# Scatters into the first layer's table without an order among themselves, each behind the next chunk's products on GpSimd

## The chip, the cores and the metric

The kernel runs on one core of a Trainium2 chip. The metric is the device time of one execution in microseconds (us). A profile of one execution stands beside the timed runs; its times count from the start of its span. TensorE is called PE here, VectorE DVE, ScalarE ACT, GpSimd POOL and SyncE SP, as in the profile.

## What is computed

A decayed linear attention over 2 x 768 tokens feeds two mixture-of-experts layers, each with eight experts and one expert per token. The reference, cut to what matters:

```python
attn_out = _attn_ref(q, k, v, lam)                 # blocks of tokens, a running state per head
x = attn_out.transpose(0, 2, 1, 3).reshape(B * S, H * D)      # 1536 x 512
# first layer
xn = x / (norm(x) + 1e-6); en = expert_emb / (norm(expert_emb) + 1e-6)
logits = xn @ en.T / tau
expert_idx = argmax(logits, axis=1)
gate_w = softmax(logits)[arange(N), expert_idx]
for e in range(8):
    mask = expert_idx == e
    h = maximum(x[mask] @ w1[e], 0)                # 512 -> 1024
    out[mask] = gate_w[mask, None] * (h @ w2[e])   # 1024 -> 512
# second layer: the same with its own weights and logits = x @ w_gate
```

## The kernel before

**Attention, in steps.** A loop over `s` from 0 to 11 takes the tokens in chunks of 128 (two batches in turn). The code is written out as a hand-made software pipeline, and every engine runs its instructions in the order in which the code emits them. In step `s`, `st_A(s)` puts the products of keys and queries on PE (line 420), `st_pool(s)` puts three products on POOL (`qd` L433, the decayed queries; `kd` L437, the decayed keys; `ds` L444, the decayed state), `st_mask(s)` applies the decay mask on DVE, `st_B(s - 1)` multiplies on PE with `qd` of the chunk before (L456) and with the masked products (L461), and `st_S(s - 1)` updates the state (L475, L481). So POOL's `qd` of chunk 6 is wanted by PE in step 7. The chunk's finished rows go to a table `xd` in device memory (`st_rows`, L501, an SP transfer).

**Routing, inside the steps.** `st_lT`, `st_pick` and `st_rank` compute for each token of an earlier chunk its expert and its place in that expert's list (`posk`). Every third step from 5 on (steps 5, 8, 11) `Gates` makes the gate values of three chunks on ACT and DVE, and then `scat(it)` (L550) writes for each of the three chunks 128 records of two words, token number and gate, to rows `posk[:, it]` of the table `tab1` in device memory. It is an indirect transfer that POOL issues. The framework sees three writes into one tensor and makes each wait for the one before; the wait stands on POOL. The scatters of chunks 9 to 11 (`LATE`) come after the loop.

**Who reads the table.** `tb0` (L615, SP) loads the first 216 rows of the first expert at the end of step 11. The tokens of chunks 9 to 11 reach the first expert by matrix products (`late_in`, L584), the others by gathers of `xd` with `tb0` (L636, POOL), which PE transposes (L655). The other experts' rows come by `load_x` (L747, SP) and `gather` (L768, POOL), transposed by `x_in` (L788).

**Weights.** SP loads the experts' weights in pieces of 512 KB (`raw`, L354) into five buffers. ACT makes the upper part `whi` (L361), and DVE or POOL the rest (`wlo` L379, `wlr` L373). In the attention steps a piece is loaded at the end of a step and converted by ACT at the end of the next.

**A helper of the second layer.** `put` declares that a scatter has no dependence on the scatters before it, keeps it in a list, and puts a one-element `memset` of `gap` behind it on POOL. `after_puts` makes a reader of the table wait for all of that list. Before the change only scatters into the second layer's table (L960) use them.

Of the kernel before, what the change touches and what calls it, by code (L numbers as in the profile page):

```python
# [75 lines left out]
def body(ctx, tc, nc, A, O):  # L76
# [5 lines left out]
    tab1 = dram.tile([E * TS, 2], I32, name="tab1")  # L82
    tab2 = dram.tile([E * TS, 3], I32, name="tab2")
    F_d = dram.tile([8, 256], F32, name="F_d")
    tab1_e = tab1.rearrange("(e n) r -> e n r", e=E)
# [6 lines left out]
    rec1 = const.tile([128, 12, 2], I32, name="rec1")  # L92
# [9 lines left out]
    posk = const.tile([128, 12], I32, name="posk")  # L102
# [97 lines left out]
    for g in range(2):  # L200
        nc.sync.dma_start(
            out=Dm[:, 4 * g:4 * g + 4, :],
            in_=bass.AP(tensor=f0.tensor, offset=f0.offset + 256 * g, ap=[[1, 128], [512, 4], [1, 128]]))
    load_X(1, 1)
    qtab = ac.tile([128, 4, 128], F32, name="qtab")
    for hh in range(2):
        nc.sync.dma_start(out=qtab[64 * hh:64 * hh + 64],
                          in_=bass.AP(tensor=f0.tensor, offset=f0.offset + 256 * hh + 128,
                                      ap=[[0, 64], [512, 4], [1, 128]]))
# [60 lines left out]
        nc.vector.tensor_copy(out=enT[:, :, 0:8], in_=pe)  # L270


    puts = []
    gap = const.tile([1, 1], F32, name="gap")

    def put(inst):

        for p in puts:
            tc.declare_no_dep(inst.ins, p.ins, reason="distinct rows")
        puts.append(inst)  # L280
        nc.gpsimd.memset(gap, 0.0)

    def after_puts(inst):
        for p in puts:
            tc.add_manual_dep(inst.ins, p.ins.name, mybir.DependencyInfo(mybir.DependencyClass.Sync, mybir.DependencyReason.DATA), reason="rows of the table")

    def route_pick(lg, n, nb, inv=None):
# [140 lines left out]
    def st_pool(it):  # L428
        b, c = it % 2, it // 2
        X = Xs[it]  # L430
        if c > 0:
            qd = wk.tile([128, 4, 128], F32, tag="qd", name="qd")
            nc.gpsimd.tensor_tensor(out=qd, in0=X[:, 0, :].rearrange("p (a i) -> p a i", a=4), in1=qtab, op=ALU.mult)  # L433
            qds[it] = qd
        if c < 5:
            kd = wk.tile([128, 512], F32, tag="kd", name="kd")
            nc.gpsimd.tensor_tensor(  # L437
                out=kd.rearrange("p (a g d) -> p g a d", g=2, d=64),
                in0=X[:, 2, :].rearrange("p (a g d) -> p g a d", g=2, d=64),
                in1=Dm[:, :, 127:128].rearrange("p (g a) o -> p g a o", g=2).to_broadcast([128, 2, 4, 64]), op=ALU.mult)  # L440
            kds[it] = kd
        if 0 < c < 5:
            ds = wk.tile([128, 4, 64], F32, tag="ds", name="ds")
            nc.gpsimd.tensor_tensor(out=ds, in0=state[b][c % 2], in1=qtab[:, :, 127:128].to_broadcast([128, 4, 64]),  # L444
                                    op=ALU.mult)
            dss[it] = ds
# [100 lines left out]
            route_gate(self.sh, 128, self.n, rec1[:, self.s, 1:2].bitcast(F32))  # L547

    def scat(it):
        nc.gpsimd.indirect_dma_start(out=tab1[:, :], out_offset=bass.IndirectOffsetOnAxis(ap=posk[:, it:it + 1], axis=0),  # L550
                                     in_=rec1[:, it, :], in_offset=None)

    lTs = {}
    Ps = {}
# [10 lines left out]
    W0, nb0 = W1S[0], nblk(W1S[0])  # L565
    n0 = W0 // nb0
# [17 lines left out]
            nc.tensor.matmul(pt0[k // 2][:, k % 2, :], xrs[it][:, 128 * k:128 * k + 128], Ps[it],  # L584
                             start=(it == LATE[0] and k % 2 == 0), stop=False)

    gates = None
    for s in range(12):
        ps = psf[s] if s < 2 else st_A(s)
        st_pool(s)  # L590
        if s >= 3:
            st_rank(s - 3)
        if s >= 5 and s % 3 == 2:
            gates = Gates(s - 5, s - 2)
        st_mask(s, ps, 0)
        st_mask(s, ps, 1)
        if s >= 2:
            st_lT(s - 2)
            st_rows(s - 2)
        if gates:  # L600
            gates.shift()
            gates.exp()
        if s >= 1:
            st_B(s - 1)
            st_S(s - 1)
        if gates:
            gates.gate()
            for it in range(s - 5, s - 2):
                scat(it)
            gates = None  # L610
        if s >= 2:
            st_pick(s - 2)
        if s == 11:
            tb0 = sm.tile([n0, nb0, 2], I32, tag="tb0", name="tb0", bufs=1)
            nc.sync.dma_start(out=tb0, in_=tab1_e[0, 0:W0, :].rearrange("(j p) c -> p j c", p=n0))  # L615
        if 1 <= s and s + 3 < 12:
            load_X(s + 3)
        if s == 1:
            init_dram()
        if s >= 5:  # L620
            wcur.load(s - 5)
        for g in LO_AT.get(s, ()):
            wcur.split_lo(g)
        if 6 <= s < 11:
            wcur.split_hi(wcur.todo.pop(0))
# [22 lines left out]
    gates = Gates(9, 12)  # L648
# [78 lines left out]
    class Expert:  # L727
# [12 lines left out]
        def load_x(self):  # L740
            n, nb, W = self.n, self.nb, self.W
            self.tb = sm.tile([n, nb, self.nc_], I32, tag="tb", name="tb", bufs=4)
            if isinstance(self.e, int):
                src = self.tab[self.e, 0:W, :].rearrange("(j p) c -> p j c", p=n)
            else:
                src = self.tab[bass.ds(self.e, 1), 0:W, :].rearrange("a (j p) c -> p (a j) c", p=n)
            i = nc.sync.dma_start(out=self.tb, in_=src)  # L747
            if self.second:
                after_puts(i)
            self.gate = self.tb[:, :, self.nc_ - 1:self.nc_].bitcast(F32)  # L750

        def begin(self):
# [576 lines left out]
```

## Time and profile before

| | us |
|---|---|
| median of 3 runs | 499.51 (494.91 to 502.37) |
| the profiled execution, its own time | 493.88 |
| its span, first to last instruction | 492.1 |
| PE busy | 433.0 (88% of the span) |
| DVE busy | 336.9 (68%) |
| ACT busy | 269.7 (55%) |
| POOL busy | 226.1 (46%) |

The time of the profiled execution is its span and 1.8 us around it. Busy time is that of compute instructions alone; an engine that waits in its queue counts as idle. The steps of the attention take about the first 92 us, the experts the rest.

### The profile page before, as it was taken

To read this page: it belongs to the slowest core of one execution; us is meant where nothing else is said; L and a number is where in the kernel's file an instruction comes from. 1 tells how busy PE (TensorE), PEld (TensorE's weight loads), DVE (VectorE), ACT (ScalarE), POOL (GpSimd) and SP (SyncE) were. 2 spreads that over 40 slices of the span, in tenths; PEclk is the share of its full clock that TensorE was granted. 3 is DMA by queue.
4 is the path that set the end of the run, shared out by engine and by line. 5 is a ranking of instruction groups with operands and counts; after the bars stand their busy time and mean duration, and the time that the engine had idled before them with its cause. 6 is when DMAs were issued, how large, how long until landed. Compare 5 with 4: busy or idle time off the path is not lost. (4 is left out here: it accounts for less than half of the span.)

```text
span 492.1 us, 9560 instructions
## 1 busy us (share of the span) xinstructions
PE 433.0 (88%) x3482; PEld 375.2 (76%) x3484; DVE 336.9 (68%) x714; ACT 269.7 (55%) x443; POOL 226.1 (46%) x224
## 2 busy tenths in 40 slices
PE   7696577759699999999999898999999999999980
PEld 3585566549578898988888797878987788988970
DVE  5454282525569888989888966853858588989950
ACT  2244253404467575665767445645768585776830
POOL 4641725415262738375574634403435725545520
PEclk9999697978899999999999999999999999999996
DMA  6998283231958485867658246483767767786400
GB/s 199 338 345 291 96 291 75 52 125 10 356 173 281 159 283 168 286 188 264 221 190 277 85 170 206 139 259 129 260 213 247 268 206 250 245 265 244 152 25 15
DMA packets 36693, 99.00 MB, mean 201 GB/s; under 512 B 10524, under 2 KB 12068, under 8 KB 35617
## 3 DMA queue, kind: packets, MB, share of 16 engines
q1 hardware_dynamic: 31569, 88.02, 53.7%
q0 software_dynamic: 4768, 10.28, 6.7%
q8 instruction: 29, 0.48, 0.4%
q14 instruction: 23, 0.19, 0.1%
q10 hardware_dynamic: 304, 0.03, 0.0%
HBM read 87.65 MB, written 11.21 MB: 201 GB/s over the span
## 5 line engine op out<-in xcount | busy, mean ns | idle before, releaser
L379 DVE SCALAR_TENSOR_TENSOR wlo<-raw,whi 128x1024 f16<-128x1024 f32 x98 | 128.8, 1316 | 33.0 <-ACT whi L361 32.1
L361 ACT ACTIVATE whi<-raw 128x1024 fp32r<-128x1024 f32 x128 | 131.3, 1050 | 5.2 <-DMA raw<-in_wa_dram 5.2
L373 POOL TENSOR_TENSOR wlr<-raw,whi 128x1024 fp32r<-128x1024 f32 x30 | 73.7, 2457 | 112.3 <-ACT whi L361 90.1
L795 PE MATMUL pm<-xT,whi 128*128 128x416 f32 (+8 forms) x416 | 99.2, 364 | 6.7 <-DVE xT L577 3.2
L795 PE MATMUL pm<-ht,whi 128*128 128x416 f32 (+7 forms) x384 | 86.7, 362 | 0.0
L795 PEld LDWEIGHTS pm<-xT,whi 128*128 128x128 f32 x416 | 68.8, 189 | 12.4 <-DVE xT L577 5.1
L795 PEld LDWEIGHTS pm<-ht,whi 128*128 128x128 f32 x384 | 66.8, 191 | 2.0
L801 PEld LDWEIGHTS <-wlo 128*128 128x128 f16 x720 | 57.2, 98 | 14.0 <-issue 8.6
L801 PE MATMUL pm<-xH,wlo 128*128 128x208 f16 (+11 forms) x512 | 59.4, 259 | 0.6 <-DVE xH L580 0.6
L845 ACT ACTIVATE ht<-t 128x416 fp32r<-128x416 f32 (+11 forms) x64 | 35.9, 561 | 27.4 <-DVE t L839 27.1
L851 DVE SCALAR_TENSOR_TENSOR ht<-t,ht 128x416 fp32r<-128x416 f32 (+11 forms) x64 | 42.6, 666 | 7.9 <-ACT ht L845 7.9
L838 ACT ACTIVATE t<-pm 128x416 f32<-128x416 f32 (+8 forms) x52 | 26.3, 506 | 33.9 <-PE pm L795 33.7
L839 DVE SCALAR_TENSOR_TENSOR t<-pm,t 128x416 f32<-128x416 f32 (+8 forms) x52 | 29.7, 571 | 14.8 <-ACT t L838 14.1
L960 POOL DMA_INDIRECT tab<-rec,pi x16 | 27.8, 1739 | 21.1 <-issue 7.3
L550 POOL DMA_INDIRECT tab<-rec,posk x12 | 11.9, 995 | 46.9 <-DMA tab<-rec,posk 25.4
L801 PE MATMUL pm<-ht,wlr 128*128 128x208 f32 (+8 forms) x208 | 33.4, 282 | 0.0
L967 POOL DMA_INDIRECT out_y_dram<-yr,tb x17 | 19.3, 1137 | 30.0 <-ACT yr L928 21.5
L574 ACT ACTIVATE xT<-pt 128x384 fp32r<-128x384 f32 (+9 forms) x33 | 16.8, 513 | 23.8 <-PE pt L788 11.9
L801 PEld LDWEIGHTS pm<-ht,wlr 128*128 128x128 f32 x208 | 29.1, 190 | 0.4
L768 POOL DMA_INDIRECT xr<-y2d,tb x17 | 24.1, 1416 | 9.3 <-issue 7.5
L801 PE MATMUL pm<-hh,wlo 128*128 128x208 f16 (+8 forms) x208 | 26.2, 256 | 0.0
L768 POOL DMA_INDIRECT xr<-xd,tb x14 | 23.4, 1670 | 4.4 <-issue 3.1
(197 smaller groups left out, 715.5 us busy)
## 6 DMA issues: line engine op xcount, KB each, us to landing
raw<-in_wa_dram SPq DMA_DIRECT2D x64, 512.0 KB, 5.5
raw<-in_wb_dram SPq DMA_DIRECT2D x64, 512.0 KB, 4.1
X<-in_att_dram SPq DMA_DIRECT2D x8, 1024.0 KB, 7.7
X<-in_att_dram SPq DMA_DIRECT2D x8, 512.0 KB, 6.1
xd<-xr SPq DMA_DIRECT2D x12, 256.0 KB, 4.6
y2d<-yr SPq DMA_DIRECT2D x2, 416.0 KB
y2d<-yr SPq DMA_DIRECT2D x2, 384.0 KB, 3.3
Dm<-F_d SPq DMA_DIRECT2D x2, 256.0 KB
```

Source lines behind the costliest of these rows:

```text
L361: nc.scalar.activation(out=f, in_=self.raw[g], func=AF.Copy, scale=self.scale(g))
L373: (nc.gpsimd if self.pat[g] == "p" else nc.vector).tensor_tensor(out=t.rearrange("p a b -> p (a b)"), in0=self.raw[g], in1=self.hi[g].rear ...
L379: nc.vector.scalar_tensor_tensor(out=t.rearrange("p a b -> p (a b)"), in0=self.raw[g], scalar=SW, in1=self.hi[g].rearrange("p a b -> p (a ...
L768: nc.gpsimd.indirect_dma_start(out=xr[0:n], out_offset=None, in_=self.rows, in_offset=bass.IndirectOffsetOnAxis(ap=idx[:, j, 0:1], axis=0))
L795: nc.tensor.matmul(pm[:, j, 0:2 * W].rearrange("p (a w) -> p a w", a=2), wh, s2, start=first, stop=last)
L801: nc.tensor.matmul(pm[:, j, 0:self.W], wl, sh, start=False, stop=False)
L838: nc.scalar.activation(out=t1, in_=pm[:, :, W:2 * W], func=AF.Copy, scale=sc)
L839: nc.vector.scalar_tensor_tensor(out=t2, in0=pm[:, :, 0:W], scalar=sc, in1=t1, op0=ALU.mult, op1=ALU.add)
L845: nc.scalar.activation(out=ht[:, :, 0, :], in_=t2, func=AF.Relu)
L851: nc.vector.scalar_tensor_tensor(out=ht[:, :, 1, :], in0=t2, scalar=0.0, in1=ht[:, :, 0, :].bitcast(F32), op0=ALU.max, op1=ALU.subtract)
L960: i = nc.gpsimd.indirect_dma_start(out=tab2[:, :], out_offset=bass.IndirectOffsetOnAxis(ap=self.pi[:, j:j + 1], axis=0), in_=rec2[0:n, rb[ ...
L967: i = nc.gpsimd.indirect_dma_start(out=O["y"], out_offset=bass.IndirectOffsetOnAxis(ap=self.tb[:, j, 1:2], axis=0), in_=self.yr[0:n, j, :] ...
```

## The change

The scatters into `tab1` go through `put` with a list of their own (`puts1`), so they don't wait for one another, and a `gap` memset stands behind each. The three scatters of a group are no longer issued together in the step in which their gates are made: they are put in a list `ready`, and each of the next three steps issues one, behind that step's `st_pool`. In step 11 those that are left are issued on the spot. `tb0` and every later load of rows of `tab1` wait for all scatters issued by then.

```diff
-    puts = []
+    puts, puts1 = [], []
     gap = const.tile([1, 1], F32, name="gap")
-    def put(inst):
-        for p in puts:
+    def put(inst, to=puts):
+        for p in to:
             tc.declare_no_dep(inst.ins, p.ins, reason="distinct rows")
-        puts.append(inst)
+        to.append(inst)
         nc.gpsimd.memset(gap, 0.0)
...
     def scat(it):
-        nc.gpsimd.indirect_dma_start(out=tab1[:, :], out_offset=bass.IndirectOffsetOnAxis(ap=posk[:, it:it + 1], axis=0),
-                                     in_=rec1[:, it, :], in_offset=None)
+        put(nc.gpsimd.indirect_dma_start(
+            out=tab1[:, :], out_offset=bass.IndirectOffsetOnAxis(ap=posk[:, it:it + 1], axis=0),
+            in_=rec1[:, it, :], in_offset=None), puts1)
...
-    gates = None
+    gates, ready = None, []
     for s in range(12):
         ps = psf[s] if s < 2 else st_A(s)
         st_pool(s)
+        if ready:
+            scat(ready.pop(0))
...
             gates.gate()
-            for it in range(s - 5, s - 2):
-                scat(it)
+            ready += range(s - 5, s - 2)
             gates = None
+            while s == 11 and ready:
+                scat(ready.pop(0))
...
-            nc.sync.dma_start(out=tb0, in_=tab1_e[0, 0:W0, :].rearrange("(j p) c -> p j c", p=n0))
+            after_puts(nc.sync.dma_start(out=tb0, in_=tab1_e[0, 0:W0, :].rearrange("(j p) c -> p j c", p=n0)), puts1)
...
             i = nc.sync.dma_start(out=self.tb, in_=src)
-            if self.second:
-                after_puts(i)
+            after_puts(i, puts if self.second else puts1)
```

The instructions of PE, DVE and ACT and their order stay as they were. Three places show what moves. The first is POOL's queue from the end of step 5 to step 8 before the change; `tab` is the table, `rec` the records, `DMASW` the semaphores of POOL's own transfers.

```order
L444 TENSOR_TENSOR ds<-st_183,qtab 128x256 [waits DVE_49]
L550 DMA tab_62<-rec_69,posk 13312x2 [waits DVE_49]
L550 DMA tab_62<-rec_69,posk 13312x2 [waits DMASW0_49]
L550 DMA tab_62<-rec_69,posk 13312x2 [waits DMASW1_49]
L433 TENSOR_TENSOR qd<-X,qtab 128x512 [waits DMAHW4_49,PE_49,Pool_49]
L437 TENSOR_TENSOR kd<-X,Dm 128x2x4x64 [waits PE_49,Pool_49]
L444 TENSOR_TENSOR ds<-st_182,qtab 128x256 [waits Pool_49]
```

The same engine and the same place after the change:

```order
L444 TENSOR_TENSOR ds<-st_183,qtab 128x256 [waits DVE_49]
L433 TENSOR_TENSOR qd<-X,qtab 128x512 [waits DMAHW4_49,PE_49,Pool_49]
L437 TENSOR_TENSOR kd<-X,Dm 128x2x4x64 [waits PE_49,Pool_49]
L444 TENSOR_TENSOR ds<-st_182,qtab 128x256 [waits DVE_49]
L550 DMA tab_62<-rec_69,posk 13312x2 [waits DVE_49]
L281 MEMSET gap 1x1
L433 TENSOR_TENSOR qd<-X,qtab 128x512 [waits DMAHW6_49,PE_49,Pool_49]
L437 TENSOR_TENSOR kd<-X,Dm 128x2x4x64 [waits PE_49,Pool_49]
L444 TENSOR_TENSOR ds<-st_184,qtab 128x256 [waits DVE_49]
L550 DMA tab_62<-rec_69,posk 13312x2
L281 MEMSET gap 1x1 [waits Pool_49]
```

The products of chunk 6 stood behind three scatters, of which two waited for a transfer; now they stand ahead of the first, and one scatter follows each chunk's products.

The second place is POOL's queue around the end of step 11, before the change; L636 is the first gather for the first expert, L373 a product of weights.

```order
L433 TENSOR_TENSOR qd<-X,qtab 128x512 [waits DMAHW1_49,PE_49,Pool_49]
L550 DMA tab_62<-rec_69,posk 13312x2 [waits DMASW5_49,DVE_49]
L550 DMA tab_62<-rec_69,posk 13312x2 [waits DMASW6_49]
L550 DMA tab_62<-rec_69,posk 13312x2 [waits DMASW7_49]
L373 TENSOR_TENSOR wlr<-raw,whi 128x1024 [waits DMAHW4_49,Activation_49]
L636 DMA xr<-xd,tb_1179 108x512 [waits DMAHW5_49,DMAHW3_49,DMAHW7_49,DMAHW2_49,DMAHW0_49]
```

After the change:

```order
L433 TENSOR_TENSOR qd<-X,qtab 128x512 [waits DMAHW1_49,PE_49]
L550 DMA tab_62<-rec_69,posk 13312x2
L281 MEMSET gap 1x1 [waits Pool_49]
L550 DMA tab_62<-rec_69,posk 13312x2 [waits DVE_49]
...
L550 DMA tab_62<-rec_69,posk 13312x2 [waits DMASW0_49]
...
L373 TENSOR_TENSOR wlr<-raw,whi 128x1024 [waits DMAHW4_49,Activation_49]
L640 DMA xr<-xd,tb_1188 108x512 [waits DMAHW3_49,DMAHW5_49,DMAHW2_49,DMAHW7_49,DMAHW0_49,DMASW1_49]
```

(Left out are the third group's second scatter, like the first row of its kind, and the `gap` rows.) The last scatter of the second group has come here, ahead of the third group, whose scatters now wait only for DVE and for transfers of much earlier scatters. The `LATE` scatters change in the same way, without moving.

The third place is SP's queue at the load of `tb0`, as a piece of the difference:

```order
 L354 DMA raw<-in_wa_dram 128x1024 [waits DMAHW6_49,DVE_49]
 L501 DMA xd<-xr 128x512 [waits DMAHW7_49,Activation_49]
-L615 DMA tb_1179<-tab_62 108x2x2 [waits DMAHW0_49,DMASW0_49]
+L619 DMA tb_1188<-tab_62 108x2x2 [waits DMASW5_49,DMASW4_49,DMASW6_49,DMASW3_49,DMASW7_49,DMASW2_49,DMAHW0_49,DMASW1_49,DMASW0_49]
 L354 DMA raw<-in_wa_dram 128x1024 [waits DMAHW1_49,DVE_49]
 L501 DMA xd<-xr 128x512 [waits DMAHW2_49,Activation_49]
```

It keeps its place, ahead of a load of weights and of the store of a chunk's rows, and waits for nine scatters in place of the last.

## Rows read from the trace of the kernel before

**Rows 1.** The page, part 2: TensorE's granted clock, 40 slices of 12.3 us.
```profile
PEclk9999697978899999999999999999999999999996
```

**Rows 2.** Waits from 20 to 125 us: who waited for whom, total, times, longest (us).
```profile
POOL tab L550 <- DMA tab<-rec,posk: 25.4, 8, 6.8
PE px L456 <- POOL qd L433: 14.3, 2, 9.5
```

**Rows 3.** Timeline of PE, 36 to 83 us: start, duration, instruction, idle ahead.
```profile
37.40 1.16 PE L420 MATMUL ps<-X 64*128 64x128 f32 x16
...
42.73 1.16 PE L420 MATMUL ps<-X 64*128 64x128 f32 x16
54.43 1.97 PE L456 MATMUL px<-qd,st 64*64 64x128 f32 x16 [9.46 <-POOL qd L433]
58.62 1.16 PE L420 MATMUL ps<-X 64*128 64x128 f32 x16
...
70.41 1.16 PE L420 MATMUL ps<-X 64*128 64x128 f32 x16
77.47 1.97 PE L456 MATMUL px<-qd,st 64*64 64x128 f32 x16 [4.83 <-POOL qd L433]
82.08 1.16 PE L420 MATMUL ps<-X 64*128 64x128 f32 x16
```

**Rows 4.** Timeline of POOL, 46 to 118 us.
```profile
46.45 0.96 POOL L550 DMA_INDIRECT tab<-rec,posk  x1 [6.79 <-DMA tab<-rec,posk]
52.12 0.97 POOL L550 DMA_INDIRECT tab<-rec,posk  x1 [4.70 <-DMA tab<-rec,posk]
53.10 1.27 POOL L433 TENSOR_TENSOR qd<-X,qtab 128x512 f32<-128x512 f32 x1
...
55.34 0.62 POOL L444 TENSOR_TENSOR ds<-st,qtab 128x256 f32<-128x256 f32 x1
...
87.38 1.01 POOL L550 DMA_INDIRECT tab<-rec,posk  x1 [5.93 <-DVE m L508]
...
92.21 0.97 POOL L550 DMA_INDIRECT tab<-rec,posk  x1 [1.44 <-DMA tab<-rec,posk]
...
100.77 1.05 POOL L636 DMA_INDIRECT xr<-xd,tb  x1 [5.20 <-issue]
...
111.82 1.00 POOL L550 DMA_INDIRECT tab<-rec,posk  x1 [8.70 <-DVE cm L694]
...
117.87 0.97 POOL L550 DMA_INDIRECT tab<-rec,posk  x1 [2.32 <-DMA tab<-rec,posk]
```

**Rows 5.** Timeline of SP's queue: the loads of table rows.
```profile
94.34 0.34 SPq L615 DMA_DIRECT2D tb<-tab  x1
...
120.03 0.41 SPq L747 DMA_DIRECT2D tb<-tab  x1
```

**Rows 6.** Timeline of PE: the first transposes of gathered rows.
```profile
104.37 0.69 PE L655 MATMUL pt<-ident,xr 108*128 108x108 f32 x4 [4.16 <-DMA xr<-xd,tb]
...
132.20 0.84 PE L788 MATMUL pt<-ident,xr 117*128 117x117 f32 x4 [4.63 <-DMA xr<-xd,tb]
```

**Rows 7.** Stretches: busy us (instructions) of each engine, clock, DMA share, GB/s.
```profile
40.00:50.00 10.00, 4.97 (x80) 4.13 (x80) 3.26 (x13) 4.34 (x9) 0.96 (x1) 0.86 0.91 297
50.00:60.00 10.00, 5.57 (x74) 5.01 (x76) 1.43 (x6) 1.93 (x4) 7.86 (x9) 0.63 0.10 33
132.00:136.00 4.00, 3.80 (x15) 3.51 (x16) 1.47 (x3) 0.98 (x2) 0.00 (x0) 0.57 0.95 354
```

**Rows 8.** Timeline of POOL, 158 to 310 us: two scatters of the second layer.
```profile
162.12 1.99 POOL L960 DMA_INDIRECT tab<-rec,pi  x1 [1.75 <-DVE xH L580]
...
164.42 2.13 POOL L960 DMA_INDIRECT tab<-rec,pi  x1 [0.21 <-PE pm L795]
```

**Rows 9.** Line 379 from 40 to 120 us: duration in ns, min/median/max.
```profile
L379 DVE SCALAR_TENSOR_TENSOR wlo<-raw,whi x6: 1214/1220/2653, 59.5 to 119.1; 128x1024 f16<-128x1024 f32 x6
```

**Rows 10.** Timeline of ACT, 44 to 47 us: a conversion waits for its weights.
```profile
45.22 1.06 ACT L361 ACTIVATE whi<-raw 128x1024 fp32r<-128x1024 f32 x1 [2.56 <-DMA raw<-in_wa_dram]
```

More of the change, by code (lines that the diff above doesn't have):

```diff
@@ L270, in prep_emb_b, with after_puts @@
         nc.vector.tensor_copy(out=enT[:, :, 0:8], in_=pe)
-    puts = []
+    puts, puts1 = [], []
     gap = const.tile([1, 1], F32, name="gap")
-    def put(inst):
-        for p in puts:
+    def put(inst, to=puts):
+        for p in to:
             tc.declare_no_dep(inst.ins, p.ins, reason="distinct rows")
-        puts.append(inst)
+        to.append(inst)
         nc.gpsimd.memset(gap, 0.0)
-    def after_puts(inst):
-        for p in puts:
+    def after_puts(inst, to=puts):
+        for p in to:
             tc.add_manual_dep(inst.ins, p.ins.name, mybir.DependencyInfo(mybir.DependencyClass.Sync, mybir.DependencyReason.DATA), reason="rows of the table")
```

## The prediction

> **What bounds the kernel now.** I first looked for stretches in which TensorE, the busiest engine, isn't fed. The page's row of granted clocks [rows 1] shows them without searching: apart from the kernel's end, the digit falls in slices 5 and 7 (49 to 62 and 74 to 86 us) and in slices 9 to 11 (98 to 135 us), all in the part that the change touches. The list of waits for 20 to 125 us names the first two [rows 2]: PE waited 14.3 us in two waits for `qd`, a product that POOL makes, and POOL waited 25.4 us in eight waits for a scatter to land before it could issue the next. The timelines join the two. POOL stood still for 6.79 and 4.70 us between the first three scatters; `qd` of chunk 6 began only at 53.10, when the third had been issued [rows 4]; and PE, which wanted it 9.46 us earlier, went on at 54.43 [rows 3]. The same happens with the second group, where PE waits 4.83 us until 77.47. So in steps 6 to 11 the path that sets the end runs through POOL's queue, although POOL is less than half busy in the whole. The third weak stretch is of another kind: PE waits 4.16 and 4.63 us for gathered rows [rows 6], and these gathers wait for table rows, hence for the last scatter of a group.
>
> **Part 1: `qd` no longer stands behind scatters.** The cost is read from the cadence of steps, which contains the wait and whatever follows from it. A step without a stall takes 42.73 - 37.40 = 5.33 us. Step 7 took 58.62 - 42.73 = 15.89, step 10 82.08 - 70.41 = 11.67 [rows 3]. The surplus is 10.56 + 6.34 = 16.90 us. It is more than the two waits (14.29), since after each the products ran at the lower clock: L456 takes 1.97 us there. With the change `qd` of chunk 6 needs only its inputs and PE's release of a buffer, both of which come more than a step ahead of its use. POOL's work in a step is then 53.10 to 55.96 for three products (2.9 us) [rows 4], 1.0 for a scatter, 0.1 for the memset and some 0.3 to the next instruction: 4.3 us in a step of 5.33. It keeps up, with 1 us to spare, and is still one step ahead of PE.
>
> **What is late next** is the transfers. While PE stood still, the DMA engines caught up: they were 91% busy at 297 GB/s from 40 to 50 us and 10% busy from 50 to 60 [rows 7]. Each of steps 6 to 8 asks for a chunk's inputs (1024 KB), a piece of weights (512 KB) and the store of a chunk's rows (256 KB), 1.84 MB; at 297 GB/s that is 6.2 us against a step of 5.33, at the 354 GB/s of another loaded stretch [rows 7] 5.2. ACT already waited 2.56 us for weights once, in step 7 [rows 10]. Inputs are asked for three steps ahead and have 10 us to land, and from step 9 on no more inputs are loaded. ACT's conversion has slack too: what it makes is used a step later. So I take nothing for transfers; the bounds are 0 and 4 x 2.56 = 10.2 us, all four steps 7 to 10 waiting as that one did.
>
> **Part 2: the group in step 11.** Its three scatters start at 87.38 and 92.21, first and last, 4.83 apart [rows 4]. Without waits the interval is a scatter and what follows until the next: the second layer's pairs, which have the memset, start 164.42 - 162.12 = 2.30 apart with a first scatter of 1.99 [rows 8], so 0.31 on top. With scatters of 0.97 to 1.01 the two intervals make 2.6 in place of 4.83: 2.2 us. The load of `tb0` follows the last scatter's landing (94.34, 2.13 after its start [rows 5]); behind it in SP's queue stands the store of chunk 10's rows, for which the gather at 100.77 waits; and PE then waits 4.16 for that gather [rows 4, 6]. All of the 2.2 us lies on this path. `tb0` now waits for nine scatters, but six are steps old. If DVE slows the scatters to 1.99 each, only 0.2 is left.
>
> **Part 3: the scatters of chunks 9 to 11.** First and last start at 111.82 and 117.87 [rows 4], 6.05 apart; now 2.6, so the next table load on SP, 2.16 after the last one's start, comes at 116.6 in place of 120.03 [rows 5]. Behind it wait loads of weights, and on POOL a weight product and the gather. The gather's rows are what PE misses for 4.63 us at 132.20 [rows 6]. One product on POOL between scatter and gather has an input from ACT; I take the full 3.4 us, with 0 as the other bound, since the gather lands among weight loads on DMA engines that are 95% busy [rows 7]. Of the wait 1.2 us would stay, and the clock need not fall: from 132 to 136 us PE was busy 3.80 us at 0.57 of full speed [rows 7], work that takes 3.80 x 0.57 = 2.2 at full speed. That gives 1.6 more.
>
> **What it adds.** Twelve memsets of 0.1 us on POOL, covered by its spare 1 us of a step; if that were gone, 1.2 us. POOL's work also meets DVE's at other moments. The conversion `wlo` took 2.65 us once and 1.22 otherwise [rows 9]; once it was beside POOL's products, and that slow one could vanish or others come. I put 1.5 us against the change for this (one such hit), between a gain of 1.4 and the price in rival B.
>
> **Sum:** 16.9 + 2.2 + 3.4 + 1.6 - 1.5 = 22.6 us. The experts' part, 88% and more PE work, keeps its length and only starts earlier.
>
> **Rivals.**
>
> *A. Transfers take the place of POOL.* Every step 7 to 10 waits 2.56 us for weights or inputs, as ACT did once [rows 10]. For: the busy DMA engines [rows 7]. Against: the slack of a step and more. Gain 22.6 - 10.2 = 12.4 us.
>
> *B. DVE and POOL hold each other up in every step.* For: `wlo` at 2.65 against 1.22 [rows 9], and a scatter of 1.99 against 0.97 where DVE is busy [rows 4, 8]; the change lets POOL's row run next to DVE's in each step. At 1.43 + 1.02 = 2.45 us in each of steps 6 to 11 the loss is 14.7 and the gain some 8. Against: POOL has the same products today, and most of its hits fall on small operations. The Trainium skill has a rule that speaks for this rival (SBUF — State Buffer, Who interferes with whom): a VectorE operation with two SBUF inputs and a GpSimd operation that reads SBUF exclude each other, and whichever starts first blocks the other for its whole length. By that rule `wlo` would be hit whenever it meets one of the three products.
>
> *C. Gathers land no earlier.* The table rows come sooner, but the gathers share the DMA engines with the weights, which come sooner as well; parts 2 and 3 give nothing. For: 12 us between the table load at 120.03 and PE's use at 132.20 [rows 5, 6]. Gain 16.9 - 1.5 = 15.4.
>
> *D. Slower: each scatter holds POOL until it has landed, whatever is declared.* Then POOL's step is 2.9 + 1.0 + the wait. The first two waits were 6.79 and 4.70 [rows 4], mean 5.7: 9.6 us in each of six steps, 58 against the 50.0 that they take now (37.40 to 87.38). That is 8 us slower. It decides from a wait of 50.0 / 6 - 3.9 = 4.4 us; with the mean of all eight waits, 3.2 [rows 2], it would still gain. Against: in the pairs of the second layer the next instruction starts 0.31 us after a scatter has ended [rows 8].
>
> **How the numbers follow.** The profiled execution took 493.88 us, with a span of 492.1; the three timed runs lie between 494.91 and 502.37 with a median of 499.51. I set the difference against the middle of these four, 497.2: 497.2 - 22.6 = 474.6 us. Chances: forecast 0.72; A 0.10 (484.8 us); C 0.10 (481.8); B 0.05 (489); D 0.03 (505). The range leaves out B and D and reaches over A and C, with the runs' spread on top: 486 at the upper end. At the lower end the collisions cost nothing and the slow `wlo` is gone, 3 us, and the base is the lowest time shown: 493.9 - 25.6 - 2 for a clock that stays up after 104 us as well = 466. Two per cent, about what a measurement of this kernel can tell from no change, are 10 us: forecast, A and C are faster by more, B lies within, D about within. Faster 0.93, within 0.05, slower 0.02.
>
> **What the profile of the changed kernel would show.** Part 1: no wait of PE for `qd` of over 1 us, steps 6 to 11 of 5 to 6 us each, clock digits of 9 from 20 to 95 us, and POOL's waits for scatters gone from the list. Part 2: `tb0` some 4.7 us after the group's first scatter in place of 7.0. Part 3: the next table load some 4.8 us after the first late scatter in place of 8.2, and PE's wait at L788 near 1 us. The prediction is wrong if ACT's waits for weights or PE's for inputs grow in steps 7 to 10 (A), if `wlo` is at 2 us or more in most steps (B), if PE's waits for gathered rows stay above 4 us (C), or if POOL's products start only when the scatter before them has landed (D).

## The result, and the profile after

| | before | after |
|---|---|---|
| median of 4 runs, us | 499.11 (494.91 to 502.37) | 480.0 (478.48 to 480.41) |
| the profiled execution, its own time | 493.88 | 478.48 |
| its span | 492.1 | 476.5 |

The changed kernel takes 0.964 of the time before (95% interval 0.957 to 0.970). The prediction was 474.6 us, 466 to 486, with 0.93 on faster; so the sign and the range hold, and the forecast is 5.4 us too low. Ratios here and below, and the medians of the experiments, leave disturbed executions out, so a ratio can differ from that of the two medians.

Line numbers after the change are one to four higher: L615 is now L619, L636 L640, L655 L659, L747 L751, L768 L771, L788 L791, L960 L963, L1090 L1093.

**The first 95 us.** The granted clock first, from the page, part 2, slices of 11.9 us; it answers to [rows 1].

```profile
PEclk9899999699999999999999968999999999999996
```

The low digits at 49 to 62 and 74 to 86 us are gone. One is left in slice 8 (83 to 95 us). New ones stand in slice 2 (12 to 24 us), ahead of the first step that the change touches, and in slices 24 and 25 (274 to 298 us). The list of waits from 20 to 125 us (who waited for whom: total, times, longest) has no line of PE for `qd` and none of POOL for a scatter's landing, which headed [rows 2]. What stands there now:

```profile
ACT whi L361 <- DMA raw<-in_wa_dram: 8.4, 3, 3.6
...
PE pt L659 <- DMA xr<-xd,tb: 4.2, 1, 4.2
...
PE bq L507 <- DVE sh L538: 2.3, 2, 2.0
PE pt L791 <- DMA xr<-xd,tb: 2.3, 2, 2.0
```

PE's timeline (start, duration, instruction) answers to [rows 3]; L420 opens a step.

```profile
38.16 1.16 PE L420 MATMUL ps<-X 64*128 64x128 f32 x16
...
44.62 1.16 PE L420 MATMUL ps<-X 64*128 64x128 f32 x16
...
49.62 1.16 PE L420 MATMUL ps<-X 64*128 64x128 f32 x16
...
56.74 1.16 PE L420 MATMUL ps<-X 64*128 64x128 f32 x16
...
62.40 1.16 PE L420 MATMUL ps<-X 64*128 64x128 f32 x16
...
67.39 1.16 PE L420 MATMUL ps<-X 64*128 64x128 f32 x16
```

Step 7 takes 49.62 - 44.62 = 5.00 us (15.89 before), step 10 67.39 - 62.40 = 4.99 (11.67). But step 6 takes 6.46 (5.33 before), and step 8 7.12 (6.52 before). POOL's timeline against [rows 4]: a scatter now stands behind each chunk's three products, and the groups follow one another without waits.

```profile
46.33 1.00 POOL L550 DMA_INDIRECT tab<-rec,posk  x1 [0.16 <-issue]
...
47.98 1.27 POOL L433 TENSOR_TENSOR qd<-X,qtab 128x512 f32<-128x512 f32 x1 [0.56 <-PE px L456]
49.47 1.06 POOL L437 TENSOR_TENSOR kd<-X,Dm 128x512 f32<-128x512 f32 x1 [0.21 <-PE pst L475]
...
52.31 1.00 POOL L550 DMA_INDIRECT tab<-rec,posk  x1 [0.16 <-issue]
...
72.69 0.97 POOL L550 DMA_INDIRECT tab<-rec,posk  x1 [4.41 <-DVE m L508]
...
75.24 0.97 POOL L550 DMA_INDIRECT tab<-rec,posk  x1 [0.21 <-issue]
...
84.95 1.04 POOL L640 DMA_INDIRECT xr<-xd,tb  x1 [6.33 <-issue]
...
95.99 1.01 POOL L550 DMA_INDIRECT tab<-rec,posk  x1 [8.69 <-DVE cm L698]
...
98.60 0.97 POOL L550 DMA_INDIRECT tab<-rec,posk  x1 [0.22 <-issue]
```

The three scatters of step 11 start 2.55 us apart, first and last (4.83 before), the late ones 2.61 (6.05 before): 1.28 from one to the next, as the prediction had it (1.3). SP's queue and PE's first transposes answer to [rows 5, 6]:

```profile
78.25 0.34 SPq L619 DMA_DIRECT2D tb<-tab  x1
...
88.57 4.07 PE L659 MATMUL pt<-ident,xr 108*128 108x108 f32 x16 [4.16 <-DMA xr<-xd,tb]
...
101.56 0.40 SPq L751 DMA_DIRECT2D tb<-tab  x1
...
112.51 0.62 PE L791 MATMUL pt<-ident,xr 117*128 117x117 f32 x4 [1.98 <-DMA xr<-xd,tb]
```

`tb0` is issued 5.56 us after the group's first scatter (6.96 before), the next table load 5.57 us after the first late one (8.21 before). PE's wait at L659 is 4.16 us still, that at L791 1.98 in place of 4.63.

**The balance by stretches.** With A(k) for PE's first L420 of step k, and "first put" for the first scatter of the second layer (L963; 162.12 before [rows 8], 141.35 after), the 15.6 us between the two spans are:

| stretch | before | after | gain |
|---|---|---|---|
| start to A(4) | 26.77 | 27.80 | -1.0 |
| A(4) to A(11): steps 7 and 10 | 27.56 | 9.99 | 17.6 |
| the other five steps | 27.75 | 29.60 | -1.9 |
| A(11) to the first L659 | 22.29 | 21.18 | 1.1 |
| from there to the first put | 57.75 | 52.78 | 5.0 |
| first put to the end | 329.98 | 335.15 | -5.2 |

At the first put the changed kernel was 20.8 us ahead; 5.2 of these are gone at the end, though nothing was changed there. Where they went shows at the start of the second layer, where POOL gathers the rows of its first expert. The timeline of the changed kernel, rows of DVE, POOL and PE (L379 is `wlo`, two conversions in a row):

```profile
272.49 2.36 DVE L379 SCALAR_TENSOR_TENSOR wlo<-raw,whi 128x1024 f16<-128x1024 f32 x2 [0.39 <-ACT whi L361]
...
272.70 1.84 POOL L771 DMA_INDIRECT xr<-y2d,tb  x1 [3.99 <-DMA tb<-tab]
...
274.85 0.94 POOL L771 DMA_INDIRECT xr<-y2d,tb  x1 [0.31 <-issue]
...
277.88 1.01 PE L1093 MATMUL pt<-ident,xr 112*128 112x112 f32 x4 [2.58 <-DMA xr<-y2d,tb]
```

The gather's issue took 1.84 us, beside a conversion of weights on DVE (`wlo`) that had begun 0.21 us ahead of it. PE waited 2.58 us, and the stretch from 279 to 287 us was granted 0.50 (columns as in [rows 7]):

```profile
279.00:287.00 8.00, 8.00 (x47) 7.35 (x43) 3.97 (x25) 4.74 (x8) 1.40 (x2) 0.50 0.35 114
```

0.50 is the lower of the clock's two levels, 1.2 GHz. In the kernel before, the same gather took 0.95 us, and PE waited 0.79; there `wlo` had begun 0.03 us ahead of it:

```profile
293.29 2.42 DVE L379 SCALAR_TENSOR_TENSOR wlo<-raw,whi 128x1024 f16<-128x1024 f32 x2 [0.39 <-ACT whi L361]
293.32 0.95 POOL L768 DMA_INDIRECT xr<-y2d,tb  x1 [3.80 <-issue]
...
296.88 0.67 PE L1090 MATMUL pt<-ident,xr 112*128 112x112 f32 x4 [0.79 <-DMA xr<-y2d,tb]
```

### The profile page after: what moved, and what is told of

Its sections match the earlier page's. It is cut to its first block, busy times and chain, and to the rows that moved or that the text cites. A ratio compares the mean times of both kernels' runs of the same rounds, so it can differ in the third digit from the quotient of the medians.

```text
span 476.5 us, 9573 instructions
## 1 busy us (share of the span) xinstructions
PE 432.0 (91%) x3482; PEld 375.4 (79%) x3484; DVE 334.7 (70%) x714; ACT 268.9 (56%) x443; POOL 227.2 (48%) x236
## 4 chain that ended last, share of the span: by engine, by line
PE 56%; DVE 17%; DMA 8%; issue 7%; ACT 5%; POOL 3%; SPq 1%; POOLq 0%; DVEq 0%; ACTq 0%
PE pm L798 19%; PE pm L804 11%; DVE wlo L379 5%; PE pm L828 4%; ACT whi L361 3%; DMA xr<-xd,tb 3%; PE pm L905 2%; PE pm L906 2%; PE pm L907 2%; PE pb L930 2%; DMA raw<-in_wa_dram 2%; PE pt L791 2%; PE px L461 2%; DVE xH L581 2%; PE ps L420 1%
## 5 line engine op out<-in xcount | busy, mean ns | idle before, releaser
L379 DVE SCALAR_TENSOR_TENSOR wlo<-raw,whi 128x1024 f16<-128x1024 f32 x98 | 128.4, 1314 | 31.6 <-ACT whi L361 30.8
L373 POOL TENSOR_TENSOR wlr<-raw,whi 128x1024 fp32r<-128x1024 f32 x30 | 73.6, 2453 | 111.1 <-ACT whi L361 88.8
L798 PE MATMUL pm<-ht,whi 128*128 128x416 f32 (+7 forms) x384 | 85.5, 358 | 0.0
L854 DVE SCALAR_TENSOR_TENSOR ht<-t,ht 128x416 fp32r<-128x416 f32 (+11 forms) x64 | 40.2, 629 | 7.9 <-ACT ht L848 7.9
L963 POOL DMA_INDIRECT tab<-rec,pi x16 | 28.0, 1747 | 21.1 <-issue 7.6
L970 POOL DMA_INDIRECT out_y_dram<-yr,tb x17 | 19.3, 1137 | 31.1 <-ACT yr L931 22.6
L575 ACT ACTIVATE xT<-pt 128x384 fp32r<-128x384 f32 (+9 forms) x33 | 16.8, 512 | 22.2 <-PE pt L791 9.8
L771 POOL DMA_INDIRECT xr<-y2d,tb x17 | 23.2, 1367 | 9.2 <-DMA tb<-tab 5.4
L771 POOL DMA_INDIRECT xr<-xd,tb x14 | 23.6, 1687 | 4.0 <-issue 3.8
L885 ACT ACTIVATE t<-pm 128x416 f32<-128x416 f32 (+7 forms) x24 | 12.2, 507 | 23.2 <-PE pm L798 21.9
```

Source lines behind the costliest of these rows:

```text
L373: (nc.gpsimd if self.pat[g] == "p" else nc.vector).tensor_tensor(out=t.rearrange("p a b -> p (a b)"), in0=self.raw[g], in1=self.hi[g].rear ...
L379: nc.vector.scalar_tensor_tensor(out=t.rearrange("p a b -> p (a b)"), in0=self.raw[g], scalar=SW, in1=self.hi[g].rearrange("p a b -> p (a ...
L771: nc.gpsimd.indirect_dma_start(out=xr[0:n], out_offset=None, in_=self.rows, in_offset=bass.IndirectOffsetOnAxis(ap=idx[:, j, 0:1], axis=0))
L798: nc.tensor.matmul(pm[:, j, 0:2 * W].rearrange("p (a w) -> p a w", a=2), wh, s2, start=first, stop=last)
L854: nc.vector.scalar_tensor_tensor(out=ht[:, :, 1, :], in0=t2, scalar=0.0, in1=ht[:, :, 0, :].bitcast(F32), op0=ALU.max, op1=ALU.subtract)
L963: i = nc.gpsimd.indirect_dma_start(out=tab2[:, :], out_offset=bass.IndirectOffsetOnAxis(ap=self.pi[:, j:j + 1], axis=0), in_=rec2[0:n, rb[ ...
```

## The experiments

All ratios are to the kernel before on the same chip. The stretches are read from each profile as in the balance above; "gather" is the issue of the second layer's first gather, "PE" the wait for its rows.

| kernel | ratio, 95% interval | A(4) to A(11) | A(11) to first put | first put to end | gather, PE |
|---|---|---|---|---|---|
| before | 1 | 55.3 | 80.0 | 330.0 | 0.95, 0.79 |
| before, once more | a single run | 58.0 | 80.5 | 330.8 | 0.96, 0.32 |
| after | 0.964 [0.957, 0.970] | 39.6 | 74.0 | 335.2 | 1.84, 2.58 |
| after, once more | 0.954 [0.951, 0.958] | 42.0 | 74.2 | 336.9 | 2.01, 2.95 |
| after, third time | 0.965 [0.960, 0.969] | 41.9 | 76.0 | 330.1 | 0.95, 0.52 |
| no order, old place | 0.958 [0.955, 0.962] | 44.1 | 76.7 | 330.0 | 0.95, 0.49 |
| new place, ordered | 0.978 [0.972, 0.984] | 43.8 | 81.3 | 335.8 | 1.94, 2.92 |
| gather first | 0.951 [0.947, 0.955] | 46.8 | 74.9 | 331.2 | 0.96, 0.61 |
| weights early | 0.954 [0.946, 0.961] | 42.0 | 75.1 | 334.0 | 1.71, 2.68 |
| POOL behind gates | 0.952 [0.947, 0.957] | 42.4 | 75.5 | 332.3 | 1.77, 2.86 |
| store first | 0.953 [0.948, 0.959] | 44.3 | 73.9 | 333.4 | 1.42, 2.76 |
| all four | 0.943 [0.939, 0.948] | 43.2 | 71.5 | 332.6 | 0.96, 0.62 |
| all but the gates | 0.956 [0.952, 0.960] | 42.4 | 72.3 | 331.2 | 0.95, 0.75 |

The last two and "after, third time" ran together, the four above them together, and the remaining four together. No changed kernel ran beside "gather first" to "store first". The changed kernel's own ratios, 0.954 and 0.965 on two chips, have intervals apart from each other, so a difference of 0.01 between ratios of different chips shows nothing.

**Both kernels once more.**

> The changed kernel once more. Its first trace ran 20.8 us ahead of the trace of before at the first scatter of the second layer's table (141.35 against 162.12), but only 17.3 us ahead at that layer's last such scatter and 15.6 at the end: PE waited 2.6 us for the second layer's first gathered rows and its clock fell there. Theory 'chance': how long that gather's issue on POOL takes (1.84 us in that trace, 0.95 in the one before the change) and when its rows land differ from one execution to the next; this trace shows a wait of under 1.5 us there, or at least another one, and the time lies between 476 and 481. Rival 'given back': the earlier start causes it, and the wait is again 2.3 to 2.9 us with the clock down.

> The kernel before once more, for its trace. 'Chance': the wait for the second layer's first gathered rows, 0.79 us at first, is another one here, perhaps 2 us or more. 'Given back': it is again under 1 us. Apart from this PE's two waits for qd stand here again, 8 to 11 and 4 to 6 us, and the time is 494 to 502.

Median 480.65 us against 502.78. PE's two waits for `qd` came back in the kernel before (9.70 and 7.11 us, the second above the 4 to 6 expected), and in the changed one so did the slow gather (2.01 us, PE 2.95) and the low clock. So the loss at the second layer came twice; the runs below show what decides it.

**The two halves of the change apart.** First the order alone is taken away, and the scatters stay together where they were:

```diff
-        if ready:
-            scat(ready.pop(0))
...
-            ready += range(s - 5, s - 2)
+            for it in range(s - 5, s - 2):
+                scat(it)
```

> Only the order is taken away; the three scatters of a group stand together where they stood before. Theory 'the waits on POOL': three scatters then hold POOL for 3 x 1.0 + 3 x 0.3 = 3.9 us, from about 39 to 43, and qd of chunk 6 is ready at about 44.3, when PE wants it at about 45: PE waits under 1 us, twice, and the time is that of the changed kernel within 3 us (477 to 483). Rival 'the place': qd must stand ahead of the scatters, and without that at least half of the 17 us of steps 7 and 10 comes back: 488 or more.

Then the place alone is changed, and the order stays:

```diff
-        put(nc.gpsimd.indirect_dma_start(..., in_=rec1[:, it, :], in_offset=None), puts1)
+        nc.gpsimd.indirect_dma_start(..., in_=rec1[:, it, :], in_offset=None)
```

> Only the place is changed: one scatter behind each step's products, each still waiting for the one before. 'The waits on POOL': a scatter lands 2 to 8 us after its issue, a step takes 5 to 6, so a scatter still waits some 2 us in some steps and qd of the next chunk stays ahead of PE; steps 7 and 10 lose their stalls (13 to 16 us gained), but the groups at the end of step 11 and after the loop land as late as before, which keeps back 3 to 6 us: 482 to 487. Rival 'no order does it all': PE waits for qd about as before and the time is 492 or more.

Without the order the time is 481.6 us (0.958), with the place alone 491.6 (0.978), above the 482 to 487 expected. POOL's timeline without the order, at the old place:

```profile
39.18 1.16 POOL L550 DMA_INDIRECT tab<-rec,posk  x1 [3.30 <-DVE m L508]
...
40.65 0.97 POOL L550 DMA_INDIRECT tab<-rec,posk  x1 [0.21 <-issue]
...
41.92 0.97 POOL L550 DMA_INDIRECT tab<-rec,posk  x1 [0.22 <-issue]
...
42.95 1.27 POOL L433 TENSOR_TENSOR qd<-X,qtab 128x512 f32<-128x512 f32 x1
```

Three scatters stand ahead of `qd`, and it begins 3.77 us after the first; in [rows 4] it began 6.65 us after the second. PE didn't wait for it. So either half takes away both waits for `qd`, and A(4) to A(11) is 44 us in both. The halves part after A(11): with the order the group in step 11, here in POOL's timeline, and the late scatters keep their waits, and A(11) to the first put stays at 81.3 us (80.0 and 80.5 before); without it, 76.7.

```profile
77.71 0.97 POOL L550 DMA_INDIRECT tab<-rec,posk  x1 [4.46 <-DVE m L508]
80.10 0.97 POOL L550 DMA_INDIRECT tab<-rec,posk  x1 [1.42 <-DMA tab<-rec,posk]
82.52 0.97 POOL L550 DMA_INDIRECT tab<-rec,posk  x1 [1.45 <-DMA tab<-rec,posk]
```

The theory that the waits on POOL are the cost, not the place, holds for the tails and for the sum; what the new place adds to the order's removal, 0.958 against 0.954 for the changed kernel in the same runs, these runs can't tell from nothing.

**The gather ahead of wlo.** Added to the changed kernel: a memset on POOL behind that gather, and DVE's first `wlo` of the second layer waits for it.

```diff
                     in_offset=bass.IndirectOffsetOnAxis(ap=idx[:, j, 0:1], axis=0))
+                if mark and j == 0:
+                    hold.append(nc.gpsimd.memset(gap, 0.0))
...
+            if hold:
+                tc.add_manual_dep(i.ins, hold.pop().ins.name, ...)   # i: wlo on DVE
```

> The changed kernel with one wait more: at the second layer's start the first weight conversion on DVE (wlo) waits for a memset on POOL behind the first gather of rows, so that this gather is issued first, as it was by chance in the kernel before. Theory 'who comes first': in the changed kernel the issue of this gather took 1.84 us, since wlo had begun 0.2 us ahead of it, PE waited 2.58 us and its clock fell; here the issue takes 0.95, PE waits 1 us at most, the clock stays above 0.9 from 275 to 290 us, and 4 to 5 us of the 5.2 that were lost between the last scatter of the first layer and the last of the second layer's tables come back: ratio to the kernel before 0.946 to 0.954 where the changed kernel has 0.954 to 0.964, span some 472. Rival 'transfers': the gather is late because the table rows or the gathered rows land late among loads of weights; then the issue takes 0.95 but PE still waits 1.5 us or more, and the time stays within 1.5 us of the changed kernel's. Second rival: the wait on DVE holds back what stands behind wlo (yT), and PE waits for that in place of the gather, with no gain either.

POOL, DVE and PE in its timeline:

```profile
280.52 0.96 POOL L775 DMA_INDIRECT xr<-y2d,tb  x1 [4.06 <-DMA tb<-tab]
...
281.58 2.36 DVE L381 SCALAR_TENSOR_TENSOR wlo<-raw,whi 128x1024 f16<-128x1024 f32 x2 [1.73 <-POOL gap L779]
...
281.78 1.84 POOL L775 DMA_INDIRECT xr<-y2d,tb  x1 [0.23 <-issue]
...
283.88 0.67 PE L1099 MATMUL pt<-ident,xr 112*128 112x112 f32 x4 [0.61 <-DMA xr<-y2d,tb]
```

The issue takes 0.96 us, the second gather 1.84 in its place, PE waits 0.61, and the clock stays at 1.00 from 283 to 291 us. From the fourteenth of the sixteen scatters into the second layer's table to the last it takes 19.5 us; where `wlo` is first 20.5 to 22.4, in the kernel before 18.2. So the edit gives back part of the loss and costs some 1.2 us itself. First put to the end is 331.2 us, 4.0 less than in the changed kernel's profile. That the order of the two sets how long the issue takes is shown. The time doesn't show the gain: the ratio, 0.951, lies under the changed kernel's 0.964 and 0.965 but isn't apart from its 0.954, all three on other chips, and the span, 480.3, missed the 472 expected, since A(4) to A(11) took 46.8 us here. The third profile of the changed kernel says why the loss comes and goes:

> The changed kernel once more, on the same chip as the two above, to set them against. Step 6 or step 8 of the attention at 6.5 to 8.0 us, PE's wait at the second layer's start 2.5 to 3 us, ratio 0.954 to 0.964 if the spread of the runs so far tells. A lower ratio than 0.950 would say that the four edits are worth less than they seem by other chips.

```profile
277.26 2.43 DVE L379 SCALAR_TENSOR_TENSOR wlo<-raw,whi 128x1024 f16<-128x1024 f32 x2 [0.39 <-ACT whi L361]
...
277.30 0.95 POOL L771 DMA_INDIRECT xr<-y2d,tb  x1 [3.81 <-DMA tb<-tab]
```

Here `wlo` led by 0.04 us, the gather had 0.95, and PE waited 0.52 where 2.5 to 3 were expected. In "after, once more" it led by 0.05, and the gather had 2.01. Over the ten profiles without this edit the gather took 1.42 to 2.01 us in the six in which `wlo` led by 0.05 to 0.64, and 0.95 or 0.96 in the four others, both of the kernel before among them. First put to the end takes 330.0 to 330.8 us in these four and 332.3 to 336.9 in the six. So 2 to 7 us hang on which of the two starts first, and between two executions of one program that turned by hundredths of a microsecond. Much of it goes with the clock: in "POOL behind gates", which has the 332.3, it stayed at 1.00 from 283 to 298 us, although the gather took 1.77 and PE waited 2.86; in the other five it fell. Nor does the gather's order rule the clock alone: in "all four" the gather had 0.96, and the clock from 282 to 288 us was still 0.72. Whether the changed kernel loses it more often than the one before, three profiles against two can't say.

**Steps 6 and 8: transfers or DVE and POOL?** In the changed kernel ACT waited 3.60 us for weights in step 8, and the gates' small operations on DVE were slow beside POOL's products. DVE's and POOL's timelines of the changed kernel, in step 5:

```profile
36.13 0.16 DVE L255 TENSOR_TENSOR ga<-ga 128x3 f32<-128x3 f32 x1
...
36.21 1.27 POOL L433 TENSOR_TENSOR qd<-X,qtab 128x512 f32<-128x512 f32 x1 [1.03 <-PE px L456]
...
36.33 1.18 DVE L256 TENSOR_SCALAR ga<-ga 128x3 f32<-128x3 f32 x1
```

An operation on 128x3 words took 1.18 us, until `qd` had ended; the one ahead of it took 0.16. In the kernel before and in "no order, old place" every such operation of the gates' chain took 0.16 to 0.18 us in steps 5, 8 and 11, while "new place, ordered" has 1.23 and 1.68 us among them; so the collisions come with the new place. Two kernels take one of the two, the wait for weights and the collisions, away each. The weights one step earlier:

```diff
-        if s >= 5:
-            wcur.load(s - 5)
+        if s >= 4:
+            wcur.load(s - 4)
...
-    wcur.load(7)
```

> The changed kernel with the weight pieces of the attention steps asked for one step earlier. It tests rival A of the prediction: in the changed kernel ACT waited 8.4 us in three waits for weights, the longest 3.60 us in step 8, ahead of the gates' chain, and step 8 took 7.12 us. Theory 'a part of A': with the earlier loads these waits fall below 1 us, step 8 takes 6 us, and everything behind it starts 1 to 1.5 us earlier: ratio to the kernel before lower by 0.002 to 0.003 than the changed kernel's. Rival 'only moved': the same engines carry the same bytes, so inputs (X) or the stored rows land later instead, PE or POOL waits for those, steps 6 to 11 together take the same 34 us within 0.7, and the time is the same or up to 3 us longer.

And POOL's first product in steps 6 and 9 behind the last operation of the gates:

```diff
     def st_pool(it, late=None):   # late: the gates' last operation on DVE, in steps 6 and 9
         i = nc.gpsimd.tensor_tensor(out=qd, ...)
+        if late is not None:
+            tc.add_manual_dep(i.ins, late.ins.name, ...)
```

> The changed kernel, but in steps 6 and 9 POOL's first product (qd) waits until DVE has done the last operation of the gates. It tests rival B in the small: in the changed kernel the gates' operations on DVE ran beside POOL's products, and some took 0.56 to 1.18 us in place of 0.17, step 6 took 6.46 us (5.33 before). Theory 'DVE is held up by POOL': these operations fall back to about 0.2 us, step 6 to 5.6 us or less, and the time is 0.5 to 1.5 us shorter. Rival 'POOL has no time to spare': qd comes later by the wait, PE waits for it again (more than 0.5 us in step 7 or 10), and the time is the same or 1 to 3 us longer.

With the weights early ACT waited for none of them, yet step 8 took 7.11 us. Its timeline, DVE, POOL and PE:

```profile
55.41 1.27 POOL L433 TENSOR_TENSOR qd<-X,qtab 128x512 f32<-128x512 f32 x1
...
55.52 2.20 DVE L254 TENSOR_TENSOR ga<-ss,ga 128x3 f32<-128x3 f32 x1
...
56.64 1.05 POOL L437 TENSOR_TENSOR kd<-X,Dm 128x512 f32<-128x512 f32 x1
...
58.45 0.39 PE L507 MATMUL bq<-gsum,lT 128*128 128x8 f32 x2 [2.04 <-DVE sh L538]
```

L254, on 128x3 words, was held for 2.20 us, the whole of two products, and PE waited 2.04 us behind it. With POOL behind the gates L254 took 0.16, and step 6 5.34 us (6.46 to 8.03 in the three profiles of the changed kernel), but ACT waited 6.02 us for the third piece of weights and step 8 took 9.78:

```profile
55.58 1.06 ACT L361 ACTIVATE whi<-raw 128x1024 fp32r<-128x1024 f32 x1 [6.02 <-DMA raw<-in_wa_dram]
```

So both theories were half right, and neither kernel's ratio (0.954 and 0.952) is apart from the 0.954 of the changed kernel. The traces fit two limits that lie one behind the other: whichever is taken away, the other ends last. From A(6) to A(9) it is 18.6, 20.2 and 19.3 us in the three profiles of the changed kernel, 20.1 with the weights early, 20.1 with POOL behind the gates, and 16.2 with both (in "all four", below; 19.2 in "all but the gates"). Not all of the 16.2 need be theirs: in that profile the two steps ahead were slow, 15.4 us, in which the transfers may have caught up, and where they took 14.4 ("store first", which has neither edit) A(6) to A(9) was 17.8. The Trainium skill has the second limit (SBUF — State Buffer, Who interferes with whom): a VectorE operation with two SBUF inputs and a GpSimd operation that reads SBUF exclude each other for a whole instruction. The trace agrees, with 2.20 us for 0.16 at L254, and shows more: L254 had waited since 55.52, and POOL's second product passed it all the same.

**The store ahead of tb0.** SP's load of `tb0` is put behind the store of chunk 10's rows.

```diff
-        if s == 11:
-            tb0 = sm.tile(...)
-            after_puts(nc.sync.dma_start(out=tb0, ...), puts1)
...
     st_rows(10)
+    tb0 = sm.tile(...)
+    after_puts(nc.sync.dma_start(out=tb0, ...), puts1)
```

> The changed kernel with the load of the first table rows (tb0) put behind the store of chunk 10's rows in SP's queue. It tests the path of part 2. In the changed kernel that load was issued at 78.25 us, when the group's scatters had landed, the store behind it at 79.14, though its rows were ready at 74.9, and the first gather, which waits for both, began at 84.95; PE waited 4.16 us for it. Theory 'the store is what the gather waits for': with the store at 75 to 76 us the gather begins 2 to 4 us earlier, PE's wait falls by as much (to 0.2 to 2.2 us), and the time by 1.5 to 4 us. Rival 'the table rows are what it waits for': the gather begins 0.5 us earlier at most, PE waits 3.6 us or more, and the time is the same within 1 us; then what the change left of part 2 hangs on the scatters' landing (3.0 us) alone. Third way: the gather is earlier, but PE only waits for something else behind it (rows of the next expert, or weights), and the time is the same.

SP, DVE, POOL and PE in its timeline:

```profile
78.56 0.33 SPq L501 DMA_DIRECT2D xd<-xr  x1
...
83.54 0.34 SPq L632 DMA_DIRECT2D tb<-tab  x1
...
86.18 1.22 DVE L379 SCALAR_TENSOR_TENSOR wlo<-raw,whi 128x1024 f16<-128x1024 f32 x1
86.25 2.07 POOL L639 DMA_INDIRECT xr<-xd,tb  x1 [3.93 <-issue]
...
90.96 0.74 PE L658 MATMUL pt<-ident,xr 108*128 108x108 f32 x4 [2.85 <-DMA xr<-xd,tb]
```

The store went out 2.17 us after the group's first scatter, in place of 6.45, and the gather began 9.86 us after it, in place of 12.26. But `tb0` went out only 7.15 us after it (5.56 in the changed kernel), as the scatters landed later, and the gather's issue took 2.07 us in place of 1.04: `wlo` had begun 0.07 us ahead of it, the collision of the second layer at another place. PE's wait fell from 4.16 to 2.85. So the gather had waited for the store, and now waits for the table rows; of the 2.4 us by which it began earlier the longer issue took back 1.0, 1.3 are left at PE, and the ratio doesn't show them.

**All of them.**

> All four edits of the runs before on top of the changed kernel: weight pieces a step earlier, POOL's products of steps 6 and 9 behind the gates, the first table load behind the store, the second layer's first gather ahead of wlo. Theory 'two limits, one behind the other': with the weights early alone, step 8 kept its 7.1 us, since DVE's product of 128x3 words (line 254) then stood beside two products of POOL and took 2.20 us; with the gates alone, ACT waited 6.0 us for weights and step 8 took 9.8 us. With both, line 254 takes 0.16 us, ACT waits less than 1 us, and step 8 takes 5.6 us or less; with some 1 us from the store and 4.3 us from the gather the ratio is 0.010 to 0.015 below that of the changed kernel in the same runs. Rival 'transfers alone': step 8 keeps 6.5 us or more although neither wait is there, or POOL and PE wait for inputs (X) instead; then the ratio is 0.005 to 0.010 below, from the gather and the store alone.

> The same without the wait of POOL for the gates. By 'two limits' line 254 takes 1 us or more once in steps 5 to 8, step 8 stays at 6.5 to 7.2 us, and the time is 1 to 2 us longer than that of all four edits. By the rival the two are the same within 1 us.

With all four the median is 475.41 us, with all but the gates 480.77, and the changed kernel beside them took 483.44. L254 took 0.16 us, ACT waited for no weights before 60 us, and step 8 took 5.69; without the wait for the gates L254 took 2.21 and step 8 7.11. PE's wait for the first gather fell to 1.00 us:

```profile
88.68 0.69 PE L663 MATMUL pt<-ident,xr 108*128 108x108 f32 x4 [1.00 <-DMA xr<-xd,tb]
```

0.9434 against 0.9646 in the same runs, with intervals apart: this version beats both kernels, the changed one by 2%, more than expected (0.010 to 0.015). The wait for the gates, on top of the other three, is worth 5.4 us by the medians, where 1 to 2 were expected, and there too the intervals (0.943 and 0.956) are apart. The traces don't show the difference: the profiled executions of the last two kernels are the fastest of their seven, 475.33 and 478.18 us, over 5 below their medians, so what their other executions lost is in no trace. And in the profile of all four the gain in steps 6 to 8 is spent ahead of them: A(4) to A(6) took 15.4 us (10.4 in the changed kernel), where POOL waited 5.7 us and PE 2.5 for inputs, which is a sign of the rival, 'transfers alone'.

## Why the prediction held, and where it was off

- **Part 1 (16.9 us)**: steps 7 and 10 gave 17.6, as a step without a stall took 5.00 us, and the prediction had set 5.33 for it. No wait for `qd` is left. Shown: each half of the change alone takes it away.
- **What is late next**: taken at nothing, bounds 0 and 10.2. This was the wrong value. ACT waited 8.4 us for weights in three waits, against 4.6 before, and with the collisions the other steps grew by 1.9 us. The prediction had read one such wait of ACT in the kernel before, 2.56 us in step 7; its trace has another, 1.84 us in step 10. By the prediction's own sign rival A's mechanism is there in part; removing it alone shows no gain, since rival B's stands behind it.
- **Part 2 (2.2 us)**: 1.1. The interval between scatters was right (2.55 for 2.6), but the third landed so late that `tb0` followed its start by 3.01 us in place of 2.13, which was assumed to stay; and the low clock at the gather, which the prediction's digits of 9 up to 95 us left out, stayed. PE's wait for the gather stayed too, at 4.16 us, which is the prediction's sign of rival C at this one place.
- **Part 3 and the clock (3.4 and 1.6 us)**: 5.0 in the trace. The table load came 5.57 us after the first late scatter (4.8 predicted), PE's wait 1.98 (1.2 predicted). That the sum came out is luck in part: the table load gave 2.6 us for 3.4. From the first L659 to L791 it is 27.83 us before and 23.94 after, a gain of 3.9, and from there to the first put 1.1. The clock did stay up: 1.00 from 112 to 116 us, where the rows of the kernel before have 0.57. Shown: with the order kept, this stretch and part 2 together gain nothing (81.3 us).
- **Collisions (1.5 us against)**: the term was near the right size by luck and named the wrong operation. `wlo` stayed at 1.21 to 2.47 us in 40 to 120 us; hit were operations of 128x3 words in the gates' chain, on which PE waits. They make the same 1.9 us as the transfers and can't be summed with them.
- **"The experts' part keeps its length and only starts earlier"**: beside the transfers this is the step that failed, by 5.2 us in the profile, the largest miss of the sum. What stood in its place: a gather on POOL and a conversion on DVE that start within 0.7 us of each other, with 2 to 7 us on who is first. In the third profile of the changed kernel the step held (330.1 us for 330.0), so how much of the 5.4 us between 474.6 and 480.0 is its own stays open.
- **Rivals C and D**: C (gathers no earlier) is refuted for the whole by the tails, 80 to 74 us, though it fits the first gather; D (a scatter holds POOL) by 1.28 us from one scatter to the next.

The sum by the measured terms: 17.6 - 1.9 + 1.1 + 5.0 = 21.8 against 22.6, less 5.2 at the second layer and 1.0 before A(4) that differs already ahead of the change, is the 15.6 of the spans. These are two executions. By the medians the gain is 19.1 us, and the trace of the kernel before is its fastest execution on record: against its second trace (span 498.7 us) the three spans of the changed kernel (476.5, 482.3 and 476.2) gain 22.2, 16.4 and 22.5.

## What to carry to other kernels

An order that a framework sets among writes to distinct rows costs twice: the waits themselves, and what stands behind them on the issuing engine; take the order away first, and move the writes only if a wait is still seen. When two limits lie close behind each other, an experiment that removes one can show no gain: remove both before either is called harmless. And a gain at one place shifts every later meeting of engines, so look in the later part for pairs that start within a few tenths of a microsecond and pin the order that is wanted.

## What the runs showed of the hardware

- A gather's issue on POOL (0.95 us) took 1.42 to 2.01 us when a DVE conversion with two inputs from SBUF had begun 0.05 to 0.64 us ahead of it; in all six profiles it ended 2.05 or 2.06 us after the conversion's start, some 0.85 after the first of the two conversions (1.21 us). With a lead of 0.04 us or less it took 0.95 or 0.96. In the first layer of "store first" it took 2.07 at a lead of 0.07.
- A DVE operation of 128x3 words that waits beside POOL's products can be passed by a second product that starts while it waits: 2.20 us in place of 0.16, and 2.21 in "all but the gates".
- Scatters that don't wait for one another landed later: a median of 3.6 us from issue in the changed kernel, 2.5 in the kernel before. Whether the scatters in flight or the other transfers beside them cause it isn't shown.
